# A four-layer attention and GLU training step on one core: fusing the last GLU layer, moving its weight gradients into shared PSUM sums, transposing by DMA, and pipelining the stages by block

## The chip, the cores and the metric

The kernel runs on one core of one Trainium2 chip. The metric is the device time in microseconds (us) of one execution. A verdict compares a kernel with the kernel before in runs on the same chip; only runs of the fast state are used.

Engines are called as the profile calls them: PE is TensorE, DVE is VectorE, ACT is ScalarE, POOL is GpSimd, SP is SyncE (it only issues transfers here). PEld is PE's weight loads, which overlap its matmuls. Both kernels keep the tiles that engines work on in SBUF and let matmuls sum into PSUM, in banks of 128 x 512 fp32 values; a bank is copied out before the next sum starts in it.

## The reference, cut to what matters

```python
def _A_ref(x, wqkv, wo):                       # linear attention, 32 heads of 16
    q, k, v = split_heads(x @ wqkv)
    phi = lambda t: where(t > 0, t + 1, exp(t)) + 1e-6
    pq, pk = phi(q), phi(k)
    kv = einsum("bhsd,bhse->bhde", pk, v);  z = einsum("bhsd->bhd", pk)
    o = einsum("bhqd,bhde->bhqe", pq, kv) / (einsum("bhqd,bhd->bhq", pq, z)[..., None] + 1e-6)
    return merge_heads(o) @ wo

def _B_ref(x, w_gate, w_up, w_down):           # GLU
    return (sigmoid(x @ w_gate) * (x @ w_up)) @ w_down

x = x + A(layernorm(x));  x = x + B(layernorm(x))      # layers 0 and 1
x = x + A(layernorm(x));  x = x + B(layernorm(x))      # layers 2 and 3, the same weights again
# outputs: x, and by vjp the gradients of the input, wqkv, wo, w_gate, w_up, w_down
```

There are S = 2048 tokens, D = 512 features, F = 1376 hidden features; all is bf16. Layers 0 and 2 share the attention weights and layers 1 and 3 share the GLU weights, so each weight gradient is a sum over two layers. In the text A0 and A2 are the attention layers and B1 and B3 the GLU layers, and "u, g, d" are the up, gate and down weights.

## The kernel before

It works by tiles of 128 tokens (16 tiles). The parts that the change touches:

```python
# forward GLU, one tile of 128 tokens: hidden features along the columns
for fs in range(3):                                  # 512, 512, 352 columns
    ...                                              # g_ps = h@wg, u_ps = h@wu: 4 matmuls each
    nc.scalar.activation(ssd_t[:, 0, c0:c0 + w], g_ps[:, 0:w], ACT.Sigmoid)
    nc.scalar.activation(oms[:, 0:w], g_ps[:, 0:w], ACT.Sigmoid, scale=-1.0)
    nc.vector.tensor_tensor(hh_t[:, c0:c0 + w], u_ps[:, 0:w], ssd_t[:, 0, c0:c0 + w], ALU.mult)
    nc.gpsimd.tensor_tensor(ssd_t[:, 1, c0:c0 + w], hh_t[:, c0:c0 + w], oms[:, 0:w], ALU.mult)
    if fs >= 1:
        transposes(T, fs - 1)                        # PE transposes of hh_t, copied from PSUM by ACT
...
nc.sync.dma_start(out=sv["ssd"][rows(st), :, :], in_=ssd_t[:])      # saved for the backward stage

# backward GLU, one tile: dhh = g@wd^T, then dd = dhh * saved factors,
# then 22 PE transposes of dd and copies by ACT before the 22 matmuls of dh
tps = ps_T.tile([P, 2, 4, P], BF16, name="T_ps")
for a in range(2):
    for i, fc in enumerate(fcs):
        nc.tensor.transpose(tps[0:r, a, i, :], dd[:, a, fc * P:fc * P + r], k.ident[:])
nc.scalar.copy(ddT[:, :, fcs[0]:fcs[0] + nfull, :], tps[:, :, 0:nfull, :])

# weight gradients: groups of 256 columns; the first layer stores partials, the second reloads and adds
def p2_cols_group(k, R, lhs_all, set_t, W, dwp2d, out2d, c0, final):
    if final:
        R.eng().dma_start(out=av, in_=dwp2d[:, c0:c0 + W]...)        # reload of the partial
    for half in range(2):
        ...                                          # 2 x 16 matmuls of W columns
        if not final:
            nc.scalar.copy(av[...], psv)
        else:
            nc.vector.tensor_tensor(ov[...], psv, av[...], ALU.add)
    ...                                              # store of the partial or of the result

# the order of the program, after the four forward stages
b_bwd_p1(k, 3); a_bwd_p1(k, 2); b_bwd_p2(k, R, 3, False, ...)        # p2: weight gradients
b_bwd_p1(k, 1); a_bwd_p2(k, R, 2, False); a_bwd_p1(k, 0, ...)
b_bwd_p2(k, R, 1, True, ...); a_bwd_p2(k, RT, 0, True, ...)
```

## Time and profile before

| | before |
|---|---|
| time, median of 3 runs | 1394.76 us (1394.28 to 1396.83) |
| span of the profiled run | 1393.1 us |
| matmuls | 9956 |
| PE busy | 1297.9 us, 93% |
| matmul stream (worked out below) | about 1233 us |
| span less stream | about 160 us |

From the page of the kernel before come the line of busy times, the strips of PE, of its granted clock and of the DMA engines (40 equal slices of the span, each digit the busy share in tenths), and the line of the main DMA queue (packets, MB, share of 16 engines' span):

```profile
PE 1297.9 (93%) x9956; PEld 790.1 (57%) x9956; DVE 679.9 (49%) x1468; ACT 647.3 (46%) x1168; POOL 250.5 (18%) x413
...
PE   4989899998899898998999999999999999988988
...
PEclk9999999999999999999999999999999999999999
DMA  7622334452543497547774586964568956499745
...
q1 hardware_dynamic: 246272, 253.50, 57.2%
```

From the view of groups (line, engine, operation, output and input, count, then busy us and mean ns of one): transposes on PE, their copies by ACT, and the weight gradients with their half-width, 256-column matmuls.

```profile
L730 ACT COPY ddT<-T_ps 128x1024 bf16<-128x1024 bf16 (+1 forms) x96 | 83.1, 867 | 103.4 <-PE T_ps L728 103.3
...
L833 PE MATMUL p_ps<-p_set,p_a_15354 128*128 128x256 bf16 (+1 forms) x768 | 82.5, 267 | 10.8 <-DVE dw_stg L798 10.8
...
L728 PE MATMUL T_ps<-ident,dd_t 128*128 128x128 bf16 (+1 forms) x704 | 66.4, 221 | 3.6 <-DVE dd_t L762 3.5
```

From the chain of work that ended last, near its end (start us, length us, what):

```profile
1235.63 11.10 DMA dw_stg<-dwp_wg
...
1276.84 6.91 PE p_ps L863 x32
1283.75 13.97 PE p_ps L833 x128
```

From the view of windows, the two attention forwards, GLU layer 3 forward and backward together, and the backward pass of GLU layer 1 (start:end, length, busy us of each engine with counts, then mean granted clock, DMA share, GB/s):

```profile
0.00:114.80 114.80, 91.03 (x805) 53.85 (x806) 76.81 (x206) 75.14 (x131) 33.24 (x71) 0.99 0.56 192
...
253.40:346.70 93.30, 87.19 (x782) 51.41 (x781) 62.14 (x160) 65.92 (x118) 19.36 (x26) 0.98 0.40 134
346.70:642.20 295.50, 279.33 (x1784) 147.99 (x1784) 144.78 (x276) 162.25 (x312) 66.84 (x90) 0.98 0.57 200
...
877.70:1027.80 150.10, 145.07 (x974) 76.31 (x975) 88.03 (x158) 63.67 (x110) 12.39 (x29) 1.00 0.61 206
```

How to read this. The chain shows 32 matmuls of 512 columns in 6.91 us, 216 ns each, and 128 of 256 columns in 13.97 us, 109 ns each. The Trainium skill ("TensorE: Matmul & The Clock Gate", section "Wait — 56ns, not 53.3ns?") gives a warm pitch of columns ÷ 2.4 GHz plus about 2.5 ns, which is 215.8 and 109.2 ns here; the trace agrees. So every matmul gets a price from its columns (those of 1 and 8 columns one of about 22 ns, an assumption that adds 5 us to the sum before), and the sum over a stage is its *matmul stream*: the time it would take with PE never waiting and its clock never lowered. *Lost time* is the length of a stage less its stream.

### The profile page before, as it was taken

To read this page: it belongs to the slowest core of one execution; us is meant where nothing else is said; L and a number is where in the kernel's file an instruction comes from. 1 tells how busy PE (TensorE), PEld (TensorE's weight loads), DVE (VectorE), ACT (ScalarE), POOL (GpSimd) and SP (SyncE) were. 2 spreads that over 40 slices of the span, in tenths; PEclk is the share of its full clock that TensorE was granted. 3 is DMA by queue.
4 is the path that set the end of the run, shared out by engine and by line. 5 is a ranking of instruction groups with operands and counts; after the bars stand their busy time and mean duration, and the time that the engine had idled before them with its cause. 6 is when DMAs were issued, how large, how long until landed. Compare 5 with 4: busy or idle time off the path is not lost. (4 is left out here: it accounts for less than half of the span.)

```text
span 1393.1 us, 25045 instructions
## 1 busy us (share of the span) xinstructions
PE 1297.9 (93%) x9956; PEld 790.1 (57%) x9956; DVE 679.9 (49%) x1468; ACT 647.3 (46%) x1168; POOL 250.5 (18%) x413
## 2 busy tenths in 40 slices
PE   4989899998899898998999999999999999988988
PEld 2555455556455444554665677555548675556767
DVE  6664644567533355665857400456640676611111
ACT  5857576775776544443547411444431447600000
POOL 4026654105633300002100100010010101100000
PEclk9999999999999999999999999999999999999999
DMA  7622334452543497547774586964568956499745
GB/s 273 230 103 103 149 152 158 147 177 98 201 178 143 169 326 259 175 168 237 218 230 148 181 227 149 334 217 167 172 199 248 275 169 192 143 311 261 175 122 162
DMA packets 268853, 269.77 MB, mean 194 GB/s; under 512 B 24576, under 2 KB 245184, under 8 KB 268736
## 3 DMA queue, kind: packets, MB, share of 16 engines
q1 hardware_dynamic: 246272, 253.50, 57.2%
q10 hardware_dynamic: 22464, 14.68, 3.6%
q8 instruction: 78, 1.28, 0.4%
q14 instruction: 39, 0.32, 0.1%
HBM read 144.57 MB, written 123.57 MB: 192 GB/s over the span
## 5 line engine op out<-in xcount | busy, mean ns | idle before, releaser
L730 ACT COPY ddT<-T_ps 128x1024 bf16<-128x1024 bf16 (+1 forms) x96 | 83.1, 867 | 103.4 <-PE T_ps L728 103.3
L630 POOL TENSOR_TENSOR ssd_t<-hh_t,oms 128x512 bf16<-128x512 bf16 (+1 forms) x96 | 100.6, 1052 | 83.0 <-ACT oms L628 48.4
L648 DVE SCALAR_TENSOR_TENSOR junk<-t_sb,h_ld 128x512 bf16<-128x512 f32 x64 | 46.1, 720 | 137.6 <-ACT t_sb L646 136.6
L762 DVE TENSOR_TENSOR dd_t<-dhh_ps,ssd_ld 128x512 bf16<-128x512 f32 (+1 forms) x96 | 60.4, 629 | 102.0 <-PE dhh_ps L760 102.0
L742 PEld LDWEIGHTS <-ddT 128*128 128x128 bf16 (+1 forms) x704 | 66.3, 98 | 71.4 <-issue 12.5
L468 PE MATMUL mm_ps<-wqkv,hT 128*128 128x512 bf16 x384 | 100.2, 386 | 0.5 <-DVE x_108 L601 0.4
L742 PE MATMUL dh_ps<-wuT,ddT 128*128 128x512 bf16 (+1 forms) x352 | 96.5, 382 | 3.9 <-ACT t_sb L646 0.9
L833 PE MATMUL p_ps<-p_set,p_a_15354 128*128 128x256 bf16 (+1 forms) x768 | 82.5, 267 | 10.8 <-DVE dw_stg L798 10.8
L629 DVE TENSOR_TENSOR hh_t<-u_ps,ssd_t 128x512 bf16<-128x512 f32 (+1 forms) x96 | 60.7, 634 | 65.3 <-PE u_ps L624 50.3
L760 PE MATMUL dhh_ps<-wdT,gT 128*128 128x512 bf16 (+1 forms) x384 | 87.8, 364 | 5.0 <-DMA wdT<-wdT_d 4.3
L624 PE MATMUL u_ps<-wu,hT 128*128 128x512 bf16 (+1 forms) x384 | 92.4, 361 | 0.0
L621 PE MATMUL g_ps<-wg,hT 128*128 128x512 bf16 (+1 forms) x384 | 92.0, 361 | 0.4 <-DVE ostage L530 0.4
L833 PE MATMUL p_ps<-p_set,p_a_10151 128*128 128x256 bf16 (+1 forms) x768 | 81.5, 261 | 0.9 <-DMA p_set<-sv_hdd_130 0.9
L599 PE MATMUL y_ps<-wd,hhT 128*128 128x512 bf16 (+1 forms) x352 | 81.4, 380 | 0.0
L742 PE MATMUL dh_ps<-wgT,ddT 128*128 128x512 bf16 (+1 forms) x352 | 81.3, 379 | 0.0
L833 PEld LDWEIGHTS <-p_a_15354 128*128 128x128 bf16 x768 | 68.9, 100 | 21.7 <-issue 8.4
L590 ACT COPY hhT<-hhT_ps 128x512 bf16<-128x512 bf16 (+1 forms) x96 | 49.5, 515 | 58.3 <-PE hhT_ps L587 58.1
L728 PEld LDWEIGHTS <-dd_t 128*128 128x128 bf16 (+1 forms) x704 | 50.7, 101 | 40.8 <-DVE dd_t L762 18.5
L833 PEld LDWEIGHTS <-p_a_10151 128*128 128x128 bf16 x768 | 67.2, 98 | 9.2
L728 PE MATMUL T_ps<-ident,dd_t 128*128 128x128 bf16 (+1 forms) x704 | 66.4, 221 | 3.6 <-DVE dd_t L762 3.5
L838 DVE TENSOR_TENSOR dw_stg<-p_ps,dw_stg 128x512 bf16<-128x512 f32 (+1 forms) x36 | 23.4, 653 | 87.5 <-PE p_ps L833 74.4
L1038 PE MATMUL dh_ps<-wqkvT,dkvT 128*128 128x512 bf16 x256 | 65.6, 380 | 0.0
(493 smaller groups left out, 2498.3 us busy)
## 6 DMA issues: line engine op xcount, KB each, us to landing
p_set<-sv_hdd_130 SPq DMA_DIRECT2D x15, 1024.0 KB, 7.1
p_set<-sv_hdd_119 SPq DMA_DIRECT2D x15, 1024.0 KB, 6.3
sv_ssd_118<-ssd_t SPq DMA_DIRECT2D x16, 688.0 KB, 3.1
sv_ssd_129<-ssd_t SPq DMA_DIRECT2D x16, 688.0 KB, 3.1
ssd_ld<-sv_ssd_129 SPq DMA_DIRECT2D x16, 688.0 KB, 5.5
sv_hdd_130<-dd_t SPq DMA_DIRECT2D x16, 688.0 KB, 3.9
ssd_ld<-sv_ssd_118 SPq DMA_DIRECT2D x16, 688.0 KB, 6.0
sv_hdd_119<-dd_t SPq DMA_DIRECT2D x16, 688.0 KB, 3.7
```

Of the source, the lines that this page charges most:

```text
L468: nc.tensor.matmul(ps[:], lhsT=hT[:, kc, :], rhs=k.wqkv[:, kc, n * D:(n + 1) * D], start=(kc == 0), stop=(kc == NDC - 1))
L599: nc.tensor.matmul(y_ps[:], lhsT=T["hhT"][0:r, fc, :], rhs=k.wd[0:r, fc, :], start=(fc == 0), stop=(fc == NFC - 1))
L621: nc.tensor.matmul(g_ps[:, 0:w], lhsT=hT[:, kc, :], rhs=k.wg[:, kc, c0:c0 + w], start=(kc == 0), stop=(kc == NDC - 1))
L624: nc.tensor.matmul(u_ps[:, 0:w], lhsT=hT[:, kc, :], rhs=k.wu[:, kc, c0:c0 + w], start=(kc == 0), stop=(kc == NDC - 1))
L629: nc.vector.tensor_tensor(hh_t[:, c0:c0 + w], u_ps[:, 0:w], ssd_t[:, 0, c0:c0 + w], ALU.mult)
L630: nc.gpsimd.tensor_tensor(ssd_t[:, 1, c0:c0 + w], hh_t[:, c0:c0 + w], oms[:, 0:w], ALU.mult)
L728: nc.tensor.transpose(tps[0:r, a, i, :], dd[:, a, fc * P:fc * P + r], k.ident[:])
L730: nc.scalar.copy(ddT[:, :, fcs[0]:fcs[0] + nfull, :], tps[:, :, 0:nfull, :])
L742: nc.tensor.matmul(dh_ps[:], lhsT=T["ddT"][0:r, a, fc, :], rhs=wT[0:r, fc, :], start=(i == 0), stop=(i == n_mm - 1))
L760: nc.tensor.matmul(dhh_ps[:, 0:w], lhsT=gT[:, jc, :], rhs=k.wdT[:, jc, c0:c0 + w], start=(jc == 0), stop=(jc == NDC - 1))
L833: nc.tensor.matmul(psv[:, icl, :], lhsT=lhs_all[:, st, ic * P:(ic + 1) * P], rhs=set_t[:, st, 0:W], start=(st == 0), stop=(st == NST - 1))
L1038: nc.tensor.matmul(dh_ps[:], lhsT=lhsT, rhs=k.wqkvT[:, n * NDC + c, :], start=(i == 0), stop=(i == 3 * NDC - 1))
```

## The change

Its intent: take the transposes off PE, let the last GLU layer do forward and backward in one go so that its sigmoid products are not saved and reloaded, sum the u and g gradients of both GLU layers in PSUM so that no partial of them is stored, reloaded and added, and treat blocks of 512 tokens so that one block's matmuls cover another's elementwise work. The diff replaces nearly the whole file; its core:

```diff
-        b_fwd(k, 3, lns[3], out_cb=out_cb)          # four forward stages
-        b_bwd_p1(k, 3)                              # then the backward of the last layer
+        b_both(k, 3, lns[3])                        # layer 3: forward and backward per block
...
+        for b in range(NBLK):                       # 4 blocks of 512 tokens, features on partitions
+            for fc in range(NFC):                   # 11 chunks of 128 hidden features
+                g_ps, u_ps = ...                    # 4 + 4 matmuls of 512 columns
+                nc.scalar.activation(sd[:, 0, :], g_ps[:], ACT.Sigmoid)
+                nc.scalar.activation(oms[:], g_ps[:], ACT.Sigmoid, scale=-1.0)
+                nc.vector.tensor_tensor(hh[:], u_ps[:], sd[:, 0, :], ALU.mult)
+                nc.gpsimd.tensor_tensor(sd[:, 1, :], hh[:], oms[:], ALU.mult)
+                ps = ...                            # dhh: 4 matmuls
+                nc.scalar.copy(dhh[:], ps[:])
+                nc.vector.tensor_tensor(dd[:], dhh[:]..., sd[:], ALU.mult)
+                if fc == 1 and b: down(b - 1)       # y of the block before
+                if fc == 2 and b: dh_b(k, l, b - 1, ...)   # dx of the block before
...
-        nc.tensor.transpose(...)  +  nc.scalar.copy(...)         # in nearly all places
+        k.nc.sync.dma_start_transpose(out=t[:], in_=src[c0:c0 + w, b * SB:(b + 1) * SB])
...
+def dw_cols(k, nm, base, cols, srcs, mode):         # 512 columns, 4 PSUM banks, one or two layers
+    for i, (h, src) in enumerate(srcs):
+        for st, t in pieces(k, src, c0, w):         # transposed loads, 4 tiles at a time
+            for ic in range(NDC):
+                k.nc.tensor.matmul(ps[ic][:, 0:w], lhsT=h[:, st, ic * P:(ic + 1) * P], rhs=t,
+                                   start=(i == 0 and st == 0), stop=(i == len(srcs) - 1 and st == NST - 1))
...
+        with tc.high_priority(offset=3000): a_bwd(k, 2, False)
+        ...                                         # d gradient of layer 3: low priority, "filler" for PE's gaps
+        with tc.high_priority(offset=4000): b_bwd(k, 1)
+        ...                                         # wqkv gradient of layer 2: filler
+        with tc.high_priority(offset=5000): a_bwd(k, 0, True)
+        for s in SETS:
+            for a, nm in ((0, "wu"), (1, "wg")):    # both GLU layers in one PSUM sum
+                dw_cols(k, nm, 0, s, [(h3, k.sv[3]["ddT"][a]), (h1, k.sv[1]["ddT"][a])], None)
```

Attention is also rewritten (products of weights in place of per-token work on v), and most stores go to the POOL queue.

## The prediction

> **What bounds the kernel now.** The page's first table has TensorE (PE) busy 1297.9 of 1393.1 us (93%), VectorE 49%, ScalarE 46%, GpSimd 18%; the main DMA queue has 57.2%. PE is the limit in nearly every strip slice (8s, 9s) except at the start (4 tenths), at stage changes, and near the end, where the chain of waits shows reloads of partial weight gradients of 9 to 11 us between short matmul bursts.
>
> In that chain 32 back-to-back 512-column matmuls took 6.91 us (216 ns each), 128 of 256 columns 13.97 us (109 ns). At these rates (128 columns: about 56 ns, estimated) the 9956 matmuls in the groups view need 1233 us: 3392 of 512 columns (733 us), 2048 of 256 (223), 384 of 352 (57), about 3590 of 128 (201, of which 2820 are transposes: 158), rest 19. So 160 us of the span are not streaming: 95 PE idle, the rest broken pipelines.
>
> **What the change does to PE** (counts from the diff, same rates, estimated):
> - PE transposes nearly vanish, replaced by DMA transposes: -156 us.
> - Attention is rearranged (E = h'pk and weight products replace per-token v work): about -29.
> - The last GLU chunk becomes a full overlapping 128 instead of 96: about +7.
> - Weight gradients use 512 instead of 256 columns: about -3, half the weight loads.
> - Small work: about -5.
>
> Sum: about 5180 matmuls (4600 of 512, 256 of 352, 200 of 128, 128 of one column) = 1047 us, 186 less, all on the critical path since PE bounds.
>
> **Lost time around it.** Fusing the last GLU layer removes its saved sigmoid products and a stage change. Summing u and g gradients over both layers in PSUM removes their partial stores, the reloads in the final chain, and the adds. Gradients become low-priority PE filler between pipelined blocks, so drains shrink. ScalarE loses transpose copies (T_ps 83 us, hhT 50). I keep about 100 us of loss instead of 160: start 15-20, stage changes, attention phases where VectorE has an estimated 2 us per chunk against PE's 1.9, late transposed loads.
>
> **The danger: DMA.** The main queue moved 253.5 MB in 57.2% of the span, an engine rate of about 318 GB/s. After, I count about 130 MB plain (410 us) and about 76 MB transposed. The Trainium skill (DMA: Bandwidth & Descriptors, section Latency and other measured facts) gives 261 GB/s effective for a non-contiguous DMA transpose; this trace has none to confirm it. Then the transposes take 290 us, the total is about 61% of the span, and PE stays the limit. The last gradient stage needs 512 KB per 16 matmuls (3.46 us), 152 GB/s of transposes: below that rate it becomes DMA-bound. At 130 GB/s it would add 50-80 us.
>
> **Prediction.** 1047 + about 100 = 1145 us; 8 in 10: 1085 to 1240. Faster by over 2%: 0.93; within 2%: 0.04; slower: 0.03.
>
> **What would show it.** About 5180 matmuls, under 50 of them transposes; PE busy 1060-1110 us, 92-95%; 512-column matmuls still 216 ns apart in the chain; DMA share not above about 75% in the last 200 us; chain at the end mainly dw_ps matmuls. Wrong if: PE waits before dw_ps come from the transposed set loads (crossbar too slow, or one issue queue blocked by an earlier wait); GpSimd's store issuing or VectorE paces the attention stages; or the compile-time order leaves fillers where they do not fill, so PE busy falls under 88%.

## The result, and the profile after

| | before | after |
|---|---|---|
| time, median of 4 runs each | 1395.41 us | 1331.32 us (1321.87 to 1338.67) |
| ratio | | 0.9543, 95% interval 0.95 to 0.9587 |
| span of the profiled run | 1393.1 us | 1337.0 us |
| matmuls (weight loads counted) | 9956 | 5184 |
| matmul stream | about 1233 us | about 1045 us |
| span less stream | about 160 us | about 292 us |

A ratio is the mean time of one kernel's fast runs over that of the other's of the same rounds, so it is not quite the ratio of the medians quoted. The change is faster, but the time lies outside the predicted range of 1085 to 1240 us. All four runs are fast.

The answering lines of the page after: busy times, strips, packets and the two DMA queues (q0 is the POOL queue).

```profile
PE 1118.4 (84%) x5096; PEld 501.6 (38%) x5184; DVE 613.7 (46%) x1115; ACT 392.1 (29%) x765; POOL 384.9 (29%) x558
...
PE   2985999886899999967879668888868689999787
...
PEclk9988999997899999978989989989979899999989
DMA  9624255575344351589954977538988748667974
...
DMA packets 405385, 225.21 MB, mean 168 GB/s; under 512 B 325888, under 2 KB 384320, under 8 KB 405312
...
q1 hardware_dynamic: 382304, 148.38, 48.8%
q0 software_dynamic: 23008, 75.91, 15.7%
```

The page lists 5096 matmuls and 5184 weight loads; a few matmul records are missing from the trace, and the weight loads give the true count. PE is busy for 84% where before it was 93%, and its clock strip, which before was 9 in every slice, has 8s and 7s. Of the transposes on PE, 40 are left. In place of the others 325,888 packets are under 512 bytes (24,576 before).

The matmuls themselves run as fast as foreseen. From the chain after, 49 matmuls of 512 columns in 10.74 us, 219 ns each:

```profile
788.94 10.74 PE dh_ps L531 x49
```

The stages of the kernel after, from the view of windows, in order: A0 forward, B1 forward, A2 forward, B3 forward and backward fused, A2 backward, B1 backward, A0 backward, and the tail of weight gradients.

```profile
0.00:115.70 115.70, 74.67 (x359) 31.90 (x366) 78.78 (x163) 40.70 (x66) 58.69 (x105) 0.91 0.60 175
115.70:241.70 126.00, 117.41 (x534) 52.31 (x536) 75.06 (x142) 30.24 (x49) 45.21 (x84) 0.99 0.46 150
241.70:334.30 92.60, 71.18 (x360) 31.10 (x366) 62.34 (x123) 39.41 (x65) 33.49 (x42) 0.89 0.64 157
334.30:572.80 238.50, 231.12 (x1045) 104.32 (x1064) 120.86 (x205) 90.97 (x181) 99.13 (x129) 0.99 0.39 116
572.80:749.50 176.70, 135.74 (x607) 59.72 (x618) 87.45 (x176) 52.61 (x118) 16.38 (x26) 0.90 0.84 201
749.50:907.40 157.90, 127.59 (x529) 54.65 (x539) 84.81 (x104) 72.50 (x142) 86.58 (x94) 0.91 0.64 179
907.40:1091.80 184.40, 147.81 (x643) 64.95 (x655) 82.33 (x168) 47.78 (x107) 16.38 (x25) 0.93 0.84 202
1091.80:1337.00 245.20, 212.87 (x1032) 102.63 (x1046) 22.11 (x36) 17.86 (x39) 29.03 (x53) 0.96 0.75 175
```

With the stream worked out per stage (a stage begins at its first matmul):

| stage | before: length / stream / lost | after: length / stream / lost |
|---|---|---|
| A0 forward | 114.8 / 80.1 / 34.7 | 115.7 / 61.4 / 54.2 |
| B1 forward | 138.6 / 128.8 / 9.8 | 126.0 / 115.5 / 10.6 |
| A2 forward | 93.3 / 78.7 / 14.5 | 92.6 / 61.4 / 31.1 |
| B3 forward and backward | 295.5 / 267.3 / 28.3 | 238.5 / 229.4 / 9.1 |
| all that follows | 751 / 678 / 73 | 764.2 / 578 / 186.5 |
| — A2 backward with its filler | | 176.7 / 122.5 / 54.2 |
| — B1 backward | 150.1 / 139.8 / 10.2 | 157.8 / 115.9 / 41.9 |
| — A0 backward with its filler | | 184.5 / 136.3 / 48.2 |
| — tail of weight gradients | | 245.1 / 202.9 / 42.2 |

This table is the result in one view. The change took 188 us of matmul stream away, and 132 us of lost time came back. The whole gain is in two rows: the fused stage (57 us) and B1 forward (13 us). In the attention forwards 19 and 17 us of stream went, and the stages are as long as before to within 1 us: PE did not set their pace, so its saving was worth nothing there. DVE, on the other hand, is as busy in them as before (78.8 against 76.8 us, 62.3 against 62.1), which the two window views show. In all that follows, 100 us of stream went and the time rose by 13.

Two cautions for all comparisons of stages below. The profile of the kernel after is of the slowest of its four runs (1338.67 us). And a stage is not equally long in every run even where no edit touches it: in the profiles of the experiments A0 forward then took 112 to 116 us, A2 forward 90 to 93, B1 backward 149 to 158 (the kernel after has the longest), the tail 241 to 251. A difference of a stage that lies within these is no finding.

Two more views point at what PE waits for. From the view of waits after (who waited for whom: us, times, longest):

```profile
PEld L149 <- issue: 99.5, 151, 11.5
```

```profile
PE E_ps L335 <- DVE pkst L322: 19.5, 5, 8.5
PE dq_ps L149 <- DMA gaT_t<-ga_t: 19.1, 3, 11.1
PE k_ps L149 <- DMA hT_t<-h_t: 16.7, 1, 16.7
PE dh_ps L531 <- ACT dhh_t L639: 14.3, 3, 8.1
```

No single wait of PE is large. The lost time is spread over waits on DMA, on DVE and on ACT; 99.5 us before weight loads are put down to "issue", which means that the profile names no releaser. And from the view of one tile, the transposed loads of the weight gradients (duration on the issuing queue in ns, min/median/max; then time from issue to landing in us):

```profile
L848 SPq DMA_TRANSPOSE set_t<-sv_ddT_125 x24: 1256/1788/8164, 952.0 to 1223.9; - x24
...
DMA to landing us min/median/max: 3.3/4.4/13.9
```

One such issue holds SP's queue for a median of 1788 ns and at most 8164 ns. In the trace the transposes are 80.1 MB in packets of 256 bytes that take 22.15 ns each in the mean; over 16 engines that is a rate of 185 GB/s while packets are under way, and 433 us of all 16 engines. The plain packets on the same queue run at 311 GB/s, those of the POOL queue at 362. The skill gives 261 GB/s for a non-contiguous transposing transfer and 350 to 400 for a contiguous one ("DMA: Bandwidth & Descriptors", section "Latency and other measured facts"), and calls such transfers as fast as regular ones ("Advanced Engine Details and Errata", section "X-Bar Transpose (TRN2)"). The trace does not agree with either; the measurement decides.

The clock. The records of the granted clock hold 1.0 or 0.5 and nothing between, in stretches that are multiples of 3.413 us (but for one cut off at the end). The skill states the same window of 3413 ns and the same two states ("TensorE: Matmul & The Clock Gate", section "What's actually happening"): after an idle window the clock is at half. In the trace of the kernel after, the window need not be wholly idle: each of the 29 drops follows 3.413 us in which PE was busy for at most half (0 to 50%), and each of the 28 rises a window in which it was busy for 78% or more (before, 8 of the 10 drops do). After, the clock was at half for 157 us, and PE was busy in 112 of them; before, for 34 us, busy in 31. At half rate that is, as an estimate, 56 us of matmul time that a full clock would have saved, against 16 before. So the low clock follows gaps: a gap of a few microseconds is followed by matmuls at half rate and costs more than its length.

Four theories for the missing time, which the runs below set against each other:

- *Transposes (T).* The transposing transfers are slow, hold SP's queue and fill the DMA engines, so PE waits for data.
- *Chains and small waits (C).* Blocks wait for one another: too few buffers, and engines that hand products to and fro.
- *Filler (F).* The order, built at compile time, puts the gradient matmuls where they fill nothing.
- *Clock (K).* The low clock is what stretches the stages.

### The profile page after: what moved, and what is told of

Same layout as the page of the kernel before. It is cut to its first block, busy times and chain, and to the rows that moved or that the text cites. A ratio compares the mean times of both kernels' runs of the same rounds, so it can differ in the third digit from the quotient of the medians.

```text
span 1337.0 us, 14599 instructions
## 1 busy us (share of the span) xinstructions
PE 1118.4 (84%) x5096; PEld 501.6 (38%) x5184; DVE 613.7 (46%) x1115; ACT 392.1 (29%) x765; POOL 384.9 (29%) x558
## 2 busy tenths in 40 slices
DMA packets 405385, 225.21 MB, mean 168 GB/s; under 512 B 325888, under 2 KB 384320, under 8 KB 405312
## 4 chain that ended last, share of the span: by engine, by line
PE 39%; issue 28%; DMA 12%; POOL 7%; DVE 7%; ACT 4%; SPq 2%; POOLq 0%; ACTq 0%; DVEq 0%
PE dh_ps L531 10%; PE g_ps L149 5%; PE y_ps L149 5%; PE u_ps L149 5%; PE dh_ps L780 4%; PE dhh_ps L149 3%; POOL out_dram L834 2%; PE q_ps L149 2%; PE E_ps L335 2%; PE k_ps L149 1%; DMA sh_t<-sv_s_114 1%; POOL rp_t L398 1%; DMA sh_t<-sv_hhT_111 1%; DVE ln_stats L188 1%; DMA sv_pk_116<-pkst 1%
## 5 line engine op out<-in xcount | busy, mean ns | idle before, releaser
L860 PE MATMUL dw_ps<-set_t,h_all 128*128 128x512 bf16 (+1 forms) x1006 | 214.6, 368 | 19.5 <-ACT dw_new L833 8.1
L860 PEld LDWEIGHTS <-h_all 128*128 128x128 bf16 x1024 | 100.9, 99 | 127.3 <-issue 30.6
L531 PEld LDWEIGHTS <-dd_t 128*128 128x128 bf16 x704 | 70.5, 101 | 115.3 <-issue 25.0
L531 PE MATMUL dh_ps<-wuT,dd_t 128*128 128x512 bf16 x342 | 88.0, 399 | 24.8 <-ACT dhh_t L639 14.3
L149 PE MATMUL dhh_ps<-gT_t,wdT 128*128 128x512 bf16 x342 | 86.3, 388 | 11.5 <-ACT dhh_t L639 5.5
L149 PE MATMUL g_ps<-hT_t,wg 128*128 128x512 bf16 x352 | 91.9, 384 | 3.8 <-ACT s_t L440 2.7
L149 PE MATMUL u_ps<-hT_t,wu 128*128 128x512 bf16 x352 | 91.3, 381 | 0.0
L874 PE MATMUL dw_ps<-g_all,set_t 128*128 128x512 bf16 (+1 forms) x344 | 82.9, 387 | 6.6 <-DVE dw_new L831 3.9
L531 PE MATMUL dh_ps<-wgT,dd_t 128*128 128x512 bf16 x347 | 83.0, 386 | 0.3
L496 POOL TENSOR_TENSOR sd_t<-hh_t,oms 128x512 bf16<-128x512 bf16 x44 | 51.6, 1173 | 92.0 <-DVE hh_t L495 80.9
L149 PE MATMUL dq_ps<-gaT_t,MT 128*128 128x512 bf16 x128 | 39.7, 443 | 19.1 <-DMA gaT_t<-ga_t 19.1
L780 PE MATMUL dh_ps<-wqkvT,dqT_l 128*128 128x512 bf16 x125 | 34.7, 397 | 19.1 <-DVE dkT_t L760 12.7
```

The lines of the kernel that those rows point to most:

```text
L149: i = k.nc.tensor.matmul(out, lhsT=lhs(c), rhs=rhs(c), start=(c == 0), stop=(c == n - 1))
L496: nc.gpsimd.tensor_tensor(sd[:, 1, :], hh[:], oms[:], ALU.mult)
L531: k.nc.tensor.matmul(dh_ps[:], lhsT=dds[fc][:, a, rows(j)], rhs=(k.wuT, k.wgT)[a][:, fc, :], start=(i == 0), stop=(i == 2 * NFC - 1))
L780: nc.tensor.matmul(dh_ps[:], lhsT=lhs[:, c, rows(j)], rhs=rhs(c), start=(n == 0), stop=(n == 3 * NDC - 1))
L860: k.nc.tensor.matmul(ps[ic][:, 0:w], lhsT=h[:, st, ic * P:(ic + 1) * P], rhs=t, start=(i == 0 and st == 0), stop=(i == len(srcs) - 1 and s ...
L874: k.nc.tensor.matmul(p[0:r, :], lhsT=t[:, f:f + r], rhs=g[:, st, :], start=(i == 0 and st == 0), stop=(i == len(srcs) - 1 and st == NST - 1))
```

## The experiments

Fourteen kernels ran. Each edit is against the kernel after unless stated. "Before" is always run on the same chip beside them. Times are medians of four runs; ratios are to the kernel before. Lost time is of the profiled run. "Less than the kernel after" compares medians of different sessions on several chips; the runs of the kernel after span 17 us (1322 to 1339) and its ratio is 0.9543 [0.95, 0.9587], so a difference under some 8 us is not clear of noise.

### 1. All transposing transfers made plain (wrong results on purpose)

```diff
-    nc.sync.dma_start_transpose(out=..., in_=...)        # 16 places
+    same_bytes(nc, out=..., in_=...)                     # nc.sync.dma_start of as many bytes, same places
```

> Every transposing DMA becomes a plain DMA of the same bytes on the same queue (a wrong result on purpose). The changed kernel took 1331 us, 290 us over its matmul stream of 1045 us. Theory T (the crossbar transposes, 80 MB at 185 GB/s, and their slow issue on one queue are the main cause of the lost time): 1230 us or less. Rival C (chains of ScalarE, VectorE and GpSimd inside the attention and layer-1 stages) and rival F (gradient work piled up at the end, holes before it unfilled): the transposes hide, 1290 us or more.

Measured: 1265.84 us, ratio 0.9069 [0.9043, 0.9095], 65 us less than the kernel after. The result is wrong. From the page and the view of the tile:

```profile
DMA packets 159097, 225.20 MB, mean 178 GB/s; under 512 B 11632, under 2 KB 129456, under 8 KB 158896
...
q1 hardware_dynamic: 136016, 148.37, 36.8%
```

```profile
L48 SPq DMA_DIRECT2D set_t<-sv_ddT x48: 359/359/507, 901.9 to 1169.9; - x48
```

The same 148.37 MB on the same queue now takes 36.8% of a shorter span: 464 us of 16 engines where it took 652. One issue holds the queue for 359 ns where it held it for 1788. Lost time falls from 292 to 217 us, most in A2 backward (54 to 36) and A0 backward (48 to 30), then the tail (42 to 30), B1 backward (42 to 34) and A2 forward (31 to 25). A0 forward keeps 50 of 54. So T is right in kind, and a third of the missing time; the run falls between the figures of the theories. (The 8 us of B1 backward lie within the spread of that stage.)

### 2. Only the transposed loads of the weight gradients made plain (wrong)

```diff
-        k.nc.sync.dma_start_transpose(out=t[:], in_=src[c0:c0 + w, b * SB:(b + 1) * SB])
+        same_bytes(k.nc, out=t[:], in_=src[c0:c0 + w, b * SB:(b + 1) * SB])
```

> Only the transposed loads of the weight-gradient sets (about 40 of the 80 MB) become plain DMAs of the same bytes (wrong weight gradients on purpose). Theory T, by way of contention: these loads run in front of the loads that the attention and layer-1 backward stages need, so 1270 to 1300 us. Rivals C and F: within 1% of 1331 us. If e1 gains much and this little, it is the transposes on the critical path (hT, gT, qn, pkT) that cost, not the sets.

Measured: 1310.18 us, ratio 0.9398 [0.9369, 0.9427], 21 us less, between the two figures again. The tail, which the prediction had named as the danger, gains only 5 us of its 42. As far as the two costs add, two thirds of the cost of transposes is elsewhere: in the stages that wait for a few transposed blocks before they can start or go on.

### 3. The u and g gradients of the last GLU layer no longer summed in PSUM

```diff
+        for s in SETS:
+            for a, nm in ((0, "wu"), (1, "wg")):
+                dw_cols(k, nm, 0, s, [(h3, k.sv[3]["ddT"][a])], "first")      # before b_bwd(k, 1)
...
-                dw_cols(k, nm, 0, s, [(h3, k.sv[3]["ddT"][a]), (h1, k.sv[1]["ddT"][a])], None)
+                dw_cols(k, nm, 0, s, [(h1, k.sv[1]["ddT"][a])], "last")
```

> One part of the change undone: the u and g weight gradients of the last GLU layer are no longer summed in PSUM with those of the first; they are computed on their own, stored as partial sums right after that layer's w_down gradient, and added at the end. 384 matmuls (80 us of stream) become available as filler before the first GLU layer's backward. Rival F (holes unfilled because the summing pushes this work to the end): 1260 to 1285 us. Theory T (DMA full in just those stages): 1320 us or more. Rival C alone: also a gain, since the holes take filler whatever made them.

Measured: correct, 1351.20 us, ratio 0.9687 [0.9665, 0.9709], 20 us more. The sum in PSUM is worth that much. The run was also meant to give B1 backward something to fill its gaps with, as these gradients can be computed before it. It did not: B1 backward holds 1.9 us of gradient matmuls, as without the edit, and A0 backward took 118.6 us of them. In the order of PE's instructions the work of higher priority stands first, and 23 matmuls of the d gradient that wait for it stand ahead of the rest. So F could not be tested this way, and that the time fell on the side of T (1320 us or more) says nothing for T; what fell is the idea that low priority alone makes filler.

### 4. A second buffer for rp_t, the saved reciprocal product of attention

```diff
-        rp = k.p_st.tile([P, NDC, SB], BF16, name="rp_t", bufs=1)
+        rp = k.p_st.tile([P, NDC, SB], BF16, name="rp_t")        # 2, as the pool has
```

> The attention forward's tile rp_t gets two buffers instead of one. The trace shows GpSimd waiting 6 us for the store of the previous block's rp_t before it may write the next, and ScalarE and PE behind it, in both attention forwards (54 and 34 us lost there). Rival C: 10 to 25 us less, 1306 to 1321 us. Theory T and rival F: no change beyond 0.5%.

Measured: correct, 1320.52 us, ratio 0.9478 [0.9442, 0.9515], 11 us less, as C expected. The gain is not where the buffer is used: A0 and A2 forward keep their lost time (54 and 34). It is in the stage that follows each: B1 forward loses 1.1 us where it lost 10.6, the fused stage 0.7 where it lost 9.1; these two lengths lie clear of those of the runs without the edit. The timeline of the kernel after shows the chain at the start of B1 forward (start us, length us, then in brackets the idle time before and who ended it):

```profile
117.19 3.55 POOL L398 TENSOR_TENSOR rp_t<-eq_t,rd_t 128x512 bf16<-128x512 bf16 x3 [5.76 <-DMA sv_rpT_105<-rp_t]
118.37 0.63 ACT L396 ACTIVATE rd_t<-ld_t 128x512 bf16<-128x512 f32 x1 [7.32 <-POOL rp_t L398]
119.78 1.04 PE L149 MATMUL y_ps<-M_t,qp_t 128*128 128x512 bf16 x4 [2.43 <-DVE qp_t L397]
```

With one buffer POOL waited 5.8 us for the store of rp_t; ACT, whose buffer rd_t POOL still had to read, waited 7.3 us for POOL; DVE's qp_t waited for ACT, and PE twice for qp_t, 4.8 us, among the first matmuls of B1 forward. With two buffers PE waits for none of them after B1 forward has begun. A buffer on an engine that looked idle held up the next stage.

### 5. A fourth staging buffer for finished gradients

```diff
-    junk = k.p_ln.tile([P, D], BF16, name="junk")
+    junk = k.p_ln.tile([P, D], BF16, name="junk", bufs=1)        # makes room
-    new = pool.tile([P, D], BF16, name="dw_new")
+    new = pool.tile([P, D], BF16, name="dw_new", **(dict(bufs=4) if pool is k.p_dst else {}))
```

> The staging tile of the weight gradients (dw_new) gets four buffers instead of three (and the scratch tile junk one instead of two, to fit). Each group evacuates four PSUM banks; in the trace the fourth copy waits about 3 us for the store of the first, and the next group's matmuls wait behind it: 42 us lost in the last stage, over 11 groups. Rival C (single and too few buffers make waits of a DMA round trip): the last stage loses 12 to 20 us less, in all 1310 to 1320 us. Theory T and the half-clock theory: under 5 us.

Measured: correct, 1326.42 us, ratio 0.9513 [0.9488, 0.9539], 5 us less, which by itself lies within the spread of the kernel after and is less than C expected. The tail takes 236.9 us, under the 241 to 251 of the runs without the edit, and loses 33.9 us where it lost 42.2 (C expected 12 to 20 less). A PSUM sum leaves four banks to be emptied at once; with three buffers ACT waited 16.9 us in the tail, six times, for a store of dw_new, with four not at all. Six buffers did not fit in SBUF and were not run.

### 6. One product of B1 backward moved from POOL to DVE

```diff
-                    nc.gpsimd.tensor_tensor(sh[:, 1, i, :], sh[:, 1, i, :], oms[:], ALU.mult)
+                    nc.vector.tensor_tensor(sh[:, 1, i, :], sh[:, 1, i, :], oms[:], ALU.mult)
```

> In the first GLU layer's backward the product of hhT and 1-s moves from GpSimd to VectorE. In the trace GpSimd's two products and two store issues alternate with VectorE's two dd products, each waiting for the other, about 4.6 us per two chunks where PE has 4.3 us of work at first only 1.7. Rival C: that stage (158 us, 42 lost) gets 15 to 25 us shorter, in all 1306 to 1320 us. If the stage is held by DMA (64% busy there) or by unfilled PE time alone: no change beyond 5 us.

Measured: correct, 1323.31 us, ratio 0.9478 [0.9456, 0.95], 8 us less, a little short of what C expected (1306 to 1320); B1 backward takes 144.4 us where it took 157.8. Of these 13 us the edit can claim 5 to 13: without it the stage took 149 to 158. (Experiment 11 has it at 137, experiment 4, without this edit, at 149.) DVE got 44 more instructions and is the less busy for it. The groups of DVE in that stage, first of the kernel after and then of this run:

```profile
L641 DVE TENSOR_TENSOR dd_t<-dhh_t,sh_t 128x1024 bf16<-128x1024 bf16 x44 | 39.4, 921 | 83.7 <-POOL sh_t L637 53.8 <-DMA sh_t<-sv_s_114 29.0 <-issue 0.5
...
L591 DVE SCALAR_TENSOR_TENSOR t_sb<-hb_t,c_7261,t_sb 128x512 f32<-128x512 bf16 x1 | 6.6, 6575 | 0.0
```

```profile
L641 DVE TENSOR_TENSOR dd_t<-dhh_t,sh_t 128x1024 bf16<-128x1024 bf16 x44 | 29.4, 688 | 2.4 <-ACT dhh_t L639 0.4
L637 DVE TENSOR_TENSOR sh_t<-sh_t,oms 128x512 bf16<-128x512 bf16 x44 | 17.6, 420 | 80.3 <-DMA sh_t<-sv_s 30.3 <-DMA sh_t<-sv_hhT 25.0 <-ACT oms L636 24.9
L591 DVE SCALAR_TENSOR_TENSOR t_sb<-hb_t,c,t_sb 128x512 f32<-128x512 bf16 x16 | 12.0, 750 | 0.5
```

The product takes 1160 ns on POOL and 420 ns on DVE. Besides, the same DVE instruction (L591) that takes 753 ns took 6575 ns once in the kernel after, and dd_t took 921 ns in the mean; with the product off POOL the means are 750 and 688 ns, and no single one is over 753 and 693. The skill says why ("SBUF — State Buffer", section "Who interferes with whom"): a DVE instruction with two inputs in SBUF contends with a POOL instruction that reads SBUF; the ports that they share are an exclusive lock, and the order of issue decides which one waits. These runs agree, and show that a run of POOL products can hold one DVE instruction for several of them. How much of the gain is the faster product and how much the contention, this run does not tell apart.

### 7. Gradient matmuls tied into B1 backward

This starts from experiment 3 and issues the d gradient of the third set and the u and g gradients of layer 3 chunk by chunk inside B1 backward, each piece placed after a given matmul by an ordering that needs no wait.

```diff
-            b_bwd(k, 1)
+            b_bwd(k, 1, ug3(k, h3, g3))           # ug3 yields after each 4 tiles of gradient matmuls
...
+                    if (b * NFC + fc) % 3 < 2:
+                        k.anchor = last           # the last dhh matmul; the filler is ordered behind it
+                        with k.tc.high_priority(offset=7000):
+                            next(fill, None)
```

> As e3_unsum (1351 us), but the gradient matmuls of the last GLU layer are now tied to chunks of the first GLU layer's backward by an ordering dependence, so that PE's order really has them there; in e3 the order built had only two dozen gradient matmuls in that stage, the rest after it. Rival F (the holes only need work placed in them): about 40 us less than e3, 1305 to 1315 us, with that stage's lost time under 10 us. If the stage's lost time stays or moves elsewhere (DMA contention, the same chains): 1335 us or more.

Measured: correct, 1334.13 us, ratio 0.9559 [0.9521, 0.9597]: 17 us less than experiment 3, where F expected about 40, and no better than the kernel after. B1 backward now holds 84.7 us of gradient matmuls and loses 30.9 us where it lost 39.7 in experiment 3; the rest is in A0 backward (63.2 to 42.8), which is rid of that work, less small losses elsewhere. So real filler helps, but giving up the sum in PSUM costs as much as it brings. F explains at most some 9 us of B1 backward, which is no more than this stage's spread, and not the missing time.

### 8. More PE work in the attention forwards: three idle-running matmuls per tile

```diff
+        for _ in range(3):
+            nc.tensor.matmul(z_ps[:, 8:D], lhsT=k.ident[:], rhs=h[:, 8:D], start=False, ...)
```

> In the first half of both attention forwards (32 tiles) PE gets three extra matmuls of 504 columns per tile into an unused part of the z bank: 96 matmuls, 20 us of added PE work that nothing needs. If PE's work or its throttled clock sets the pace there: 10 to 20 us slower (or faster, if the added work keeps the clock from halving: 41 us of half clock lie in the two stages). If VectorE's chain sets the pace (79 us busy against 61 us of matmul stream in the first): within 5 us of 1331.

Measured: correct, 1339.24 us, ratio 0.9605 [0.9591, 0.962], 8 us more. Each attention forward got 10.2 us of matmuls; A0 grew by 4.4 us and A2 by 3, between the two expectations. If PE were idle for want of others, they would have been free; if PE set the pace, they would have cost 10. The time at half clock in the two stages was 41 us, as before the edit, so keeping PE busier in this way did not hold the clock up. K as a cause of its own finds no support here.

### 9. Less DVE work in the attention forwards (wrong)

```diff
-        nc.vector.bn_stats(stats[:], src)
+        nc.vector.bn_stats(stats[:], src[:, 0:64])
-        nc.vector.tensor_scalar(a_t[:], e_t[:], 1.0, EPS, ALU.min, ALU.add)    # and two like it, for q
```

> VectorE work taken out of both attention forwards (wrong result on purpose): the clamp products of keys and queries are dropped and the layer-norm statistics read 64 of 512 columns, about 20 us of VectorE work per attention layer (the statistics also in front of the GLU layers). The two stages take 116 and 92 us now, against 61 us of matmul stream each. If VectorE sets their pace: 10 to 15 us less in each, in all 1300 to 1312 us. If the transposed loads or the startup set it: under 5 us each, 1322 us or more.

Measured: 1323.71 us, ratio 0.9521 [0.9486, 0.9556], 8 us less by medians and 3 by ratios, which is not clear of noise. DVE's busy time in A0 fell from 79 to 61 us and the stage by 7.7 us, to 108.0 (112 to 116 without the edit); in A2 from 62 to 51 and by 3.1, within that stage's spread. DVE sets at most part of the pace: 18 us less work gave less than 8. Experiment 14 shows it more clearly.

### 10. Plain loads of the backward stages moved from SP's queue to POOL's

```diff
-            nc.sync.dma_start(out=qp[:], in_=by_chunk(sv["qpT"], b))
+            nc.gpsimd.dma_start(out=qp[:], in_=by_chunk(sv["qpT"], b))
 # likewise rp_l, dqT_l, ha_l, and the loads of h_all and g_all
```

> In the attention backward the plain loads (qp, rp, dqT, ha) and the whole-sequence loads leave the SP queue for GpSimd's, so that they no longer stand behind the issues of transposes, which hold that queue 1.3 to 5 us each. If the queue's order is what makes theory T cost: 10 to 25 us less, in the two attention backwards and the stages beside them, 1306 to 1320 us. If the crossbar's rate itself is the limit (DMA 84% busy there): within 5 us of 1331.

Measured: correct, 1360.58 us as the median of its three fast runs (1357.80 to 1365.66), ratio 0.9777 [0.9742, 0.9812], 29 us more; neither expectation. Its fourth, profiled run (1379.30 us) fell in the slow state, so nothing is read from its stages. The thought was that plain loads stand in SP's queue behind transposes of 1.8 us each. Taking them out of it made things worse, so either the order within SP's queue is not what costs, or the loads then stand behind POOL's own stores and products, which is worse. Which of the two, the run does not tell.

### 11. Experiments 4, 5 and 6 together

> The three small gains together: rp_t with two buffers, dw_new with four, the product of the first GLU layer's backward on VectorE. Alone they read 1320.5, 1326.4 and 1323.3 us against 1331.3. If their waits are separate, the gains add: 1306 to 1311 us, and it beats both kernels. If they share the DMA queue as the limit: 1315 us or more.

Measured: correct, 1292.27 us, ratio 0.9286 [0.9248, 0.9325]. That is 39 us under the kernel after by medians, where the three alone gave 11 + 5 + 8 = 24, and the fastest correct kernel, 7% under the kernel before. The expectation (1306 to 1311) was too careful, but by ratios the gain is 0.0257 against a sum of 0.0160, and with the intervals of the five ratios that difference of 0.010 is uncertain by about 0.011 (an estimate): that they give more than their sum is not clear of noise. Three of the four stages in which it differs (B1 forward, fused, B1 backward; the fourth is the tail), from its view of windows:

```profile
116.00:232.00 116.00, 114.60 (x530) 51.73 (x532) 72.92 (x141) 28.40 (x46) 39.89 (x79) 1.00 0.50 162
...
326.60:555.90 229.30, 227.81 (x1043) 103.55 (x1061) 118.88 (x204) 89.23 (x178) 93.76 (x124) 1.00 0.39 120
...
733.00:869.60 136.60, 122.45 (x519) 53.09 (x528) 76.15 (x148) 69.87 (x141) 35.22 (x49) 0.94 0.69 207
```

B1 forward (116.0 us, stream 114.6) and the fused stage (229.3 us, stream 228.6) now run at the rate of their matmuls, at a clock of 1.00 throughout. B1 backward takes 136.6 us where experiment 6 alone left 144.4, and the tail 233.1 where experiment 5 alone left 236.9. The clock was at half for 115 us in all where the kernel after had 157.

### 12. The last GLU layer as two stages again

```diff
-        b_both(k, 3, lns[3])
+        b_fwd(k, 3, lns[3], None)                 # stores s and hh, as layer 1 does
...
+        b_bwd(k, 3)                               # reloads them
```

> The headline of the change undone: the last GLU layer runs forward and backward as two stages again, with the functions that the first GLU layer uses (sigmoid stored and loaded, all blocks forward, then all backward). The fused stage takes 238.5 us, of which 229 are matmul stream; before the change the two stages took 295.5 us with 267 of stream. If fusing is what closed the holes: 30 to 50 us slower, 1360 to 1380 us. If the stage was good only because its transposes left PE: within 15 us of 1331.

Measured: correct, 1389.58 us, ratio 0.998 [0.9959, 1.0001], 58 us more and beyond what was expected (30 to 50): without the fusion the rest of the change brings nothing that these runs can measure. The two stages, from the view of windows, and the waits of the second; for comparison the fused stage is the row that begins at 334.30 above:

```profile
336.00:456.00 120.00, 117.14 (x535) 52.59 (x537) 58.11 (x100) 29.50 (x48) 35.58 (x60) 0.99 0.50 151
456.00:634.00 178.00, 126.32 (x520) 52.92 (x529) 90.87 (x105) 68.94 (x133) 84.11 (x89) 0.87 0.70 210
```

```profile
DVE dd_t L662 <- POOL sh_t L658: 74.7, 16, 25.1
...
PE dhh_ps L150 <- DMA gT_t<-in_grad_out_dram: 19.9, 1, 19.9
```

298 us where the fused stage took 238.5, for the same stream of 229.4 us. The forward half runs well; the backward half takes 178 us at a clock of 0.87. It begins with 19.9 us of waiting for a transposed load, and then DVE waits for the product on POOL, as in B1 backward. Fused, the matmuls of g, u and dhh and those of the block before stand ready for PE, and nothing is reloaded: its gaps stay short and its clock at 0.99. Part of the 58 us belongs to this way of splitting, then: the kernel before did the two halves as two stages in 295.5 us with 38 us more of stream.

### 13. The combination of 11 with all transposes plain (wrong)

> The three waits of the combination (39 us) and the transposes (65 us) were found by runs that each left the other in place. Theory 'separate costs': they lie in different places, so they add: 1331 - 39 - 65 = 1227 us (1217 to 1237), lost time (span less matmul stream) about 180 us. Theory 'one critical resource hides the other': removing the transposes already shortened the same waits, so the sum is smaller: 1240 to 1262. Theory 'gaps and clock feed each other': removing both also removes the half clock, so more than the sum: below 1215. Results are wrong on purpose, as the transposes no longer transpose.

Measured: 1225.68 us, ratio 0.8802 [0.8761, 0.8843]. The separate costs add as foreseen (1227; the four runs span 1221 to 1233): the small waits and the transposes are two things. Its view of windows for A0 forward, A2 backward and A0 backward:

```profile
0.00:116.00 116.00, 72.29 (x362) 31.21 (x369) 83.80 (x165) 42.63 (x69) 63.92 (x110) 0.91 0.50 175
...
548.00:703.30 155.30, 127.93 (x605) 57.96 (x616) 87.16 (x176) 51.91 (x117) 15.60 (x25) 0.95 0.69 223
...
836.60:996.60 160.00, 142.54 (x651) 64.17 (x663) 82.48 (x168) 48.30 (x108) 16.31 (x25) 0.98 0.71 232
```

A0 forward is still 116 us. Its 62 us of stream do not fill it, nor do DVE's 84 us, and transposes are not what it waits for.

### 14. The same, with less DVE work in the attention forwards (wrong)

> As the run before, and without some 20 us of VectorE work in each attention forward (worth 8 us by itself). If VectorE is the next limit there once the transposes are gone, 10 to 25 us less than the run before; if the stage is held by its start-up and the chain of dependent steps, 3 to 9 us less. If the total comes to 1180 or less, the predicted 1145 (range to 1240) was mostly lost to these named items; if it stays above 1200, at least 60 us of loss belongs to something none of the edits touches (the start of each attention stage and the chains of the attention backward stages), and the prediction was too low even with all found costs away. Results wrong on purpose.

Measured: 1212.66 us, ratio 0.8712 [0.8684, 0.874], 13 us less than experiment 13 on the same chip, as expected if DVE is the next limit there. A0 forward takes 108.9 us (7 less) and A2 forward 78.3 us (10 less, where the same edit brought 3 while transposes were slow). Still the time is not down to 1180. With all that was named taken away, 165 us are lost: 48 in A0 forward, 17 in A2 forward, 35, 18 and 23 in the three backward stages, 23 in the tail.

## Why the prediction was wrong, point by point

**The step that failed** is "I keep about 100 us of loss instead of 160". The run had 292. The other term of the sum, "about 5180 matmuls … = 1047 us", was right: 5184 and 1045.

| from the predicted 1145 us to the measured 1331 us | us | shown by |
|---|---|---|
| transposing transfers | 65 | 1; adds to the next, 13 |
| three small waits (rp_t, dw_new, product on POOL) | 39 | 11 |
| DVE work in the attention forwards | 13 | 14 |
| lost elsewhere | about 68 | left over: 1212.66 less 1145 |

The first three rows are what is gained when the thing is wholly taken away, so they bound the costs from above; of the first and the third the prediction had counted some within its 100 us ("late transposed loads", "attention phases"). The last row is open. It lies in the start and the chains of the attention stages and in what is left in the tail, at a clock that is at half for 61 us of the span; no run tells these apart. The trace of experiment 14 names the largest waits of PE that are left: 15.2 us before its first matmul in A0 forward and 10.4 for DVE's pkst there, and 13.6 for the transfer of gaT_t in A2 backward. None was tested.

**"All on the critical path since PE bounds"** was read from a share over the whole span. PE was 93% busy, yet the two attention forwards had 35 and 15 us of lost time out of 115 and 93 even before. Taking 36 us of stream from them moved their length by less than 1 us each. The saving was real where PE was at its stream: B1 forward (129 of 139) and the last GLU layer.

**"Gradients become low-priority PE filler between pipelined blocks, so drains shrink"** failed. B1 backward received 1.9 us of gradient matmuls and its lost time rose from 10 to 42 us (33 and more in every run that leaves it alone); A2 and A0 backward received about 30 and 46 us and still lost 54 and 48. A filler that stands in a fixed order fills only what comes next to it. Forced into place it gained 17 us over the same kernel without (7), and no more.

**"261 GB/s effective for a non-contiguous DMA transpose"** was mis-sized: 185. The 290 us that were estimated from it for the transposes were 433 (of 80.1 MB, where 76 were counted), and the attention backward stages had the DMA engines at 84%. Over the whole span the two queues add to 64.5%, near the 61% foreseen, but by luck: 862 us of transfers against 700 foreseen, over a span that is longer too. The average looked harmless, the stages were not. The named danger, the tail, was the smaller part (2): 21 of 65 us came from the gradient sets, and PE waited for them for only some 7 us in all. What the prediction lacked is that a few transposed blocks stand at the head of each backward stage (PE waited 19.1 us for gaT_t), and that one issue holds SP's queue for 1.8 us. Whether the rate or the issue costs more is not shown: experiment 1 takes both away, and experiment 10 did not part them.

**Fusing the last GLU layer** was right, and the largest gain that held: undone, 58 us (12), part of which is the slow way of the split. **Summing in PSUM** was right: undone, 20 us (3).

**The signs.** The prediction named its own failure: "PE busy falls under 88%" (it was 84%), and "GpSimd's store issuing or VectorE paces the attention stages" (VectorE in part, as experiment 14 shows; GpSimd's buffer, as experiment 4 shows, in the stage after). Its estimate that DVE takes 2 us per chunk against PE's 1.9 was the warning: A0 forward, with DVE busy for 79 us and a stream of 61, took 116 and ran at the pace of neither; in the sum it had no figure of its own within the 100 us.

## What to carry to other kernels

Before taking work from the busiest engine, set stream against length stage by stage: a saving in a stage that has lost time already can move into the loss, as it did in both attention forwards. Price the loss of the new kernel by its own chains, buffers and transfers rather than from the old kernel's loss, and add to each gap the half-clock matmuls after it. Giving PE several independent chains in one stage (here by fusing forward and backward) kept both gaps and clock in order, which low-priority filler in a fixed order did not.

## What the Trainium skill lacked or had wrong

- "DMA: Bandwidth & Descriptors" (261 GB/s non-contiguous, 350 to 400 contiguous) and "Advanced Engine Details and Errata" (transposes as fast as regular transfers): here 80.1 MB of transposes in 256-byte packets ran at 185 GB/s (bytes over the time of their packets, whole span), and at 208 in the tail; plain packets on the same queue at 311.
- No page gives the time that issuing one transposing transfer of this size holds SP's queue on trn2 ("DMA: Bandwidth & Descriptors" has sequencer cycles for other cases): 1256 to 8164 ns, median 1788, against 359 for a plain one of the same bytes.
- "SBUF — State Buffer" has the contention of DVE and POOL right, and could add its size in a chain: one DVE instruction of 753 ns took 6575 beside POOL products of 1160 ns.
- "TensorE: Matmul & The Clock Gate" agrees on the windows of 3.413 us, the two states and the 216 ns for 512 columns. Where it has the clock halve after an idle window, the trace of the kernel after has all 29 drops after windows in which PE was busy for 0 to 50%.
